# Seven block products in place of eight for the small terms of the last projection, in two more token groups of a GFNet + S2-MLP kernel

## The chip, the cores and the metric

The kernel runs on one core of a Trainium2 chip. The metric is the device time of one execution in microseconds (us); lower is better. The profile shown here is of one execution, and its engines are named PE (matmul), PEld (its weight load), DVE (vector), ACT (scalar), POOL (GpSimd) and SP (the queue that issues DMAs).

## The reference

The input is x, 2048 tokens by 448 features in float32. It is normalised by rows, and the output is x plus two branches on the normalised xn: a spectral filter, and a mixer with an MLP behind it.

```python
xn  = layernorm(x)
# A: global filter
yA  = irfft2(rfft2(xn) * (w_r + 1j*w_i))
# B: token shift, then MLP
h   = gelu(layernorm(xn) @ w1)                  # 448 -> 448
hs  = concat(h[:, 0:112] shifted +1, h[:, 112:224] -1, h[:, 224:336] +2, h[:, 336:448] -2)
x1  = xn + hs @ w2                              # 448 -> 448
yB  = x1 + gelu(layernorm(x1) @ w3) @ w4        # 448 -> 1792 -> 448
out = x + yA + yB
```

## The kernel before

**Split numbers.** All products run in float16 on operands split in two halves, hi and lo. A product of two split operands is three passes: hi by hi, hi by lo and lo by hi. The last two are the cross terms.

**The MLP.** The 2048 tokens stand in eight groups G of 256, and the 1792 hidden features in seven blocks fp of 256. A unit (G, fp) has a *front* (`front`, L434: 22 matmuls of 256 columns give h for 256 features and 256 tokens; then ACT takes the gelu at L772 and writes the hi half at L775, and DVE writes the lo half at L776 into the tile `hf`) and a *back* (`back`, L810: h times w4, summed in the PSUM tiles `acc` over the seven blocks). A plain back is 12 matmuls of 448 columns, 4 for each pass. `steps` is a generator that hands out fronts and backs in order, with fronts two units ahead; `run` takes from it. PSUM is taken by tags of two banks each: `mm`, `tr`, `sp` and `acc`.

**Block products.** `crossed(G, fp)` says which units form their cross terms another way; before, those of groups 5, 6 and 7 without (7, 5) and (7, 6). The cross term of a unit is a product of 2 by 2 blocks, and is made of seven block products of 128 tokens by 224 columns for each of its two passes, 14 matmuls in place of 8 of 448 columns. They need sums and differences of the blocks, here called forms: of h for each unit (`forms`, three DVE operations into the tile `hgm`, L785 to L787), and of w4 once for each block (`w4_forms`, POOL). Their sums go to four quarters of two more PSUM banks (`cr`, tag `tr`), which are added at the group's end by two ACT copies into `cross` (a part of `x2mem`) and six POOL or DVE additions.

**Around groups 1 and 2.** The same stretch also folds x for the spectral branch (`do_fold`: ACT, then four POOL operations on `xr` and `xf`), splits it (`step1_in`: `xh`, ACT hi and DVE lo, L594), multiplies it (`step1`: `ps` on PE at L603; ACT and DVE write `y`, L607 and L608), takes the largest magnitude of the filter (`w_scale`: eight loads of `wl` through two half buffers and eight DVE reductions `wm`, L269) and normalises the last four token blocks for group 6 and 7 (`ln2`: L537 to L552, tile `y`).

**What sets the order.** A tile scheduler orders each engine's instructions from priorities (`prio`; EVAC goes first, FILL last) and from hand-written lists: `behind(key)` holds an instruction in the order until another has been issued. `PACE`, `FOLD`, `WMAX` and `LATE` name for each step1 pair, fold, reduction and late normalisation the unit that it stands behind. Once built, each engine runs its own list in order, and a wait holds up all that stands behind it.

**The beginning.** Group 0 of 512 tokens goes through w1 (`w1_unit`: PE L464, ACT gelu L485, ACT hi L487, DVE lo L488, then a transposing DMA to the tile `h`, L491), and the shifted product with w2 (`w2_mm`, L509) reads those.

Of the kernel before, what the change touches and what calls it, by code (L numbers as in the profile page):

```python
# [31 lines left out]
AH = 2  # L32
PACE = [(0, 6), (1, 1), (1, 2), (1, 4), (1, 5), (2, 0), (2, 1), (2, 3)]
FOLD = [(0, 5), (1, 0), (1, 1), (1, 3), (1, 4), (1, 6), (2, 0), (2, 2)]
PIN = [("a3",), ("a3",), ("a3",), ("a3",)]
WMAX = [(1, 4), (1, 5), (2, 0), (2, 0), (2, 1), (2, 2), (2, 3), (2, 4)]
LATE = [(2, 2), (2, 3), (2, 4), (2, 5)]
HS = 3
STR = (5, 6, 7)
INV, LAG = 4, 2  # L40
EVAC, FILL = 0, 100000

# [80 lines left out]
def body(tc, nc, x, wf, w1, w2, w3, w4, c_g, c_n, c_small, out):  # L123
# [59 lines left out]
    warm = pc.tile([128, 1], F32, name="warm")  # L183
    V.memset(warm, 0.0)
    A.activation(out=warm, in_=warm, func=AF.Gelu_apprx_tanh)
    x2mem = pw.tile([128, 9 * F], F16, name="x2mem")
    wsrc = x2mem[:, 8 * F:8 * F + 512]
    V.memset(wsrc, 0.0)
    ones = pc.tile([128, 128], F32, name="ones")
# [33 lines left out]
    load_w3([2, 3])  # L223
    cross = x2mem.bitcast(F32)[:, 4 * F:4 * F + 2 * D].rearrange("p (i n) -> p i n", i=2)
    x2all = x2mem[:, 0:8 * F].rearrange("p (j t n) -> p j t n", j=4, t=7)
    w4raw = x2mem.bitcast(F32)[:, F:].rearrange("p (f n) -> p f n", f=14)
# [99 lines left out]
    def stats1(g, ks):  # L326
        if g not in mvs:
            mvs[g] = pc.tile([128, 4, 2], F32, name=f"mva{GRP[g][0]}")
        stats([xb(GRP[g][k]) for k in ks], f"a{GRP[g][ks[0]]}", mvs[g][:, ks[0]:])

    def norm1(g, apply, seen=0, mid=None):

        bs = GRP[g]
        n, b0 = len(bs), bs[0]
        stats1(g, range(seen, n))
# [140 lines left out]
    def w1_unit(g, i, pm=None):  # L476
        if pm is None:
            pm = bank(("tr" if g < 3 else "mm", "acc")[i // 2], f"pw1_{g}{i}")
            after["u", g, i] = (w1_in(g, [(i, pm)], range(4)).ins,)
        c = CS[GRP[g][i]]  # L480
        pm = pm[:, :D]
        pv_ = pm.rearrange("p (k n) -> p k n", k=4)
        h = hs_buf[c % (HS if g == 3 else HS + 2)]
        with behind(0, i - 2) if g == 0 and i > 1 else contextlib.nullcontext():
            A.activation(out=pm, in_=pm, func=AF.Gelu_apprx_tanh, scale=gsc[:, c:c + 1])  # L485
        with behind("a2") if g == 1 and i > 1 else contextlib.nullcontext():
            u = A.activation(out=h[:, 0, :, 0:112], in_=pv_, func=AF.Copy, scale=h1)  # L487
            v = V.scalar_tensor_tensor(out=h[:, 1, :, 0:112], in0=pv_, scalar=h1, in1=h[:, 0, :, 0:112],  # L488
                                       op0=ALU.mult, op1=ALU.subtract)
        o = h_at(g, i)  # L490
        d = SY.dma_start_transpose(out=hT[g][:, :, o:o + 128], in_=h.rearrange("p i k n -> p (i k n)"))  # L491
        after[g, i] = u.ins, v.ins
        after["h", g, i] = (d.ins,)
# [25 lines left out]
    def ln2(bs, engines, pins=None):  # L519
# [8 lines left out]
        for m in range(0, n, 2):  # L528
            w = stage(f"y{b0 + m}", 8 * 448, 0 if pins else (b0 + m) // 2 % 2, F16)
            o.append(w[:, 0:4 * D].bitcast(F32).rearrange("p (i n) -> p i n", i=2))  # L530
            y.append(w[:, 4 * D:8 * D].rearrange("p (i n) -> p i n", i=2))
            for i in range(2):
                e = engines[m + i]
                c = nm[:, m + i:m + i + 1]
                if e is A:
                    with behind("f", *pins[m + i]) if pins else contextlib.nullcontext():
                        A.activation(out=o[-1][:, i], in_=xb(b0 + m + i), func=AF.Identity, bias=c)  # L537
                else:
                    e.tensor_scalar(out=o[-1][:, i], in0=xb(b0 + m + i), scalar1=1.0, scalar2=c,
                                    op0=ALU.mult, op1=ALU.add)  # L540
# [27 lines left out]
    folds = {}  # L568

    def do_fold(b0):  # L570
        f = xf_buf[b0 // 2 % 4]
# [308 lines left out]
    def mlp(*args, **kw):  # L880
        run(steps(*args, **kw))
# [35 lines left out]
    def w4_split(f):  # L917
        split_w(w4p[0][:, 0, f:f + 2], w4p[0][:, 1, f:f + 2], w4raw[:, f:f + 2], s4)

    def w4_forms(fp):  # L920
        n, f = D // 2, 2 * fp
        b = [[w4p[0][:, :, f + r, n * c:n * c + n] for c in range(2)] for r in range(2)]
        m = w4all[:, 56 * 224:] if fp == 6 else w4x[:, 8 * 224 * fp:8 * 224 * (fp + 1)]
        m = m.rearrange("p (k n) -> p k n", n=224)
        t1 = [m[:, 6], m[:, 7]]
        t2, t3, t4 = (m[:, k:k + 4:3] for k in range(3))
        P.tensor_tensor(out=t3, in0=b[1][1], in1=b[0][1], op=ALU.add)
        for i in range(2):
            P.tensor_tensor(out=t1[i], in0=b[0][0][:, i], in1=b[0][1][:, i], op=ALU.subtract)
            P.tensor_tensor(out=t2[:, i], in0=b[1][1][:, i], in1=t1[i], op=ALU.subtract)  # L930
        P.tensor_tensor(out=t4, in0=b[1][0], in1=t2, op=ALU.subtract)
        w4f[fp] = [[x[:, i] for i in range(2)] for x in (b[0][0], b[1][0], b[1][1], t4)]
        w4f[fp] += [t1] + [[x[:, i] for i in range(2)] for x in (t2, t3)]

    def squares1():
        for t in range(4):
# [66 lines left out]
    with behind("a1"):  # L1003
        for k in range(4):
            w1_unit(0, k, first[k])
        n1.append(norm1(2, [P, V, A, V], 2))
    for k in (1, 3):
        with behind(0, 3):
            A.activation(out=w2p[:, 0, k], in_=w2s[:112, k], func=AF.Copy)
# [5 lines left out]
    turn(2)  # L1015
    for k in range(1, 4):
        w1_unit(1, k)
    for b, ks in ((0, (2, 0)), (1, (2, 0)), (2, (2, 0)), (3, (2,))):
        w2_mm(b, ks)
    with behind("w2p"):  # L1020
        n1[0][2]()
# [172 lines left out]
```

## Time and profile before

| | |
|---|---|
| median of 3 runs | 411.16 us (410.06 to 411.37) |
| the profiled execution | 409.13 us, of which its span is 407.0 us |
| PE busy | 401.7 us of the span (99%) |
| DVE, ACT, POOL busy | 303.6, 269.0, 178.8 us |
| granted TensorE clock | 0.999 |

PE is busy nearly from start to end. Its ends are modelled, so that one matmul of 448 columns is shown with 352 ns; how fast matmuls follow each other is read from the starts of rows of the timeline.

### The profile page before, as it was taken

To read this page: it belongs to the slowest core of one execution; us is meant where nothing else is said; L and a number is where in the kernel's file an instruction comes from. 1 tells how busy PE (TensorE), PEld (TensorE's weight loads), DVE (VectorE), ACT (ScalarE), POOL (GpSimd) and SP (SyncE) were. 2 spreads that over 40 slices of the span, in tenths; PEclk is the share of its full clock that TensorE was granted. 3 is DMA by queue.
4 is the path that set the end of the run, shared out by engine and by line. 5 is a ranking of instruction groups with operands and counts; after the bars stand their busy time and mean duration, and the time that the engine had idled before them with its cause. 6 is when DMAs were issued, how large, how long until landed. Compare 5 with 4: busy or idle time off the path is not lost.

```text
span 407.0 us, 8828 instructions
## 1 busy us (share of the span) xinstructions
PE 401.7 (99%) x3379; PEld 296.0 (73%) x3379; DVE 303.6 (75%) x658; ACT 269.0 (66%) x465; POOL 178.8 (44%) x276
## 2 busy tenths in 40 slices
PE   8999999999999999999999999999999999999996
PEld 3554555666767777776888888877788888888885
DVE  5988999898654757894577777763488879889545
ACT  4699993984838865863587888785956566544332
POOL 3889830011197747499243444441231254217100
PEclk9999999999999999999999999999999999999999
DMA  8999999906810374417055556642000022323201
GB/s 278 359 287 196 173 180 261 268 7 135 182 48 0 92 256 154 110 29 173 18 143 143 144 145 158 150 109 60 2 2 2 24 68 82 102 72 112 90 2 45
DMA packets 57209, 49.46 MB, mean 122 GB/s; under 512 B 41312, under 2 KB 52192, under 8 KB 57168
## 3 DMA queue, kind: packets, MB, share of 16 engines
q1 hardware_dynamic: 57168, 48.91, 46.1%
q8 instruction: 26, 0.43, 0.5%
q14 instruction: 15, 0.12, 0.1%
HBM read 35.06 MB, written 3.67 MB: 95 GB/s over the span
## 4 chain that ended last, share of the span: by engine, by line
PE 92%; DMA 3%; DVE 1%; POOL 1%; ACT 1%; issue 1%; SPq 0%; ACTq 0%
PE pw L434 32%; PE acc L810 24%; PE pw L509 6%; PE pw L464 6%; PE cr L825 4%; PE acc L825 3%; PE pu L706 3%; PE ps L603 3%; PE pp L660 2%; PE pe L726 2%; PE px L677 2%; PE py L748 2%; PE wps L888 2%; DMA h<-hs 2%; DMA x2mem<-w 1%; PE pta L413 1%
## 5 line engine op out<-in xcount | busy, mean ns | idle before, releaser
L434 PE MATMUL pw<-x2mem,w3p 128*128 128x256 f16 x1232 | 149.2, 272 | 0.0
L434 PEld LDWEIGHTS <-w3p 128*128 128x128 f16 x1232 | 118.8, 98 | 18.9
L810 PE MATMUL acc<-w4p,hf 128*128 128x448 f16 x508 | 107.4, 352 | 0.0
L810 PEld LDWEIGHTS <-hf 128*128 128x128 f16 x532 | 51.4, 98 | 35.5
L776 DVE SCALAR_TENSOR_TENSOR hf<-pw,h,hf 128x512 f16<-128x512 f32 x56 | 41.9, 748 | 36.6 <-ACT hf L775 36.4
L772 ACT ACTIVATE pw<-pw,pe 128x512 f32<-128x512 f32 x56 | 36.8, 657 | 44.6 <-PE pw L434 44.4
L509 PE MATMUL pw<-w2p,h 112*128 112x448 f16 x192 | 39.0, 352 | 0.3 <-DMA h<-hs 0.2
L775 ACT ACTIVATE hf<-pw,h 128x512 f16<-128x512 f32 x56 | 38.3, 684 | 1.3
L733 POOL TENSOR_TENSOR e<-e 128x226 f32<-128x226 f32 x16 | 11.2, 700 | 63.5 <-ACT e L730 60.2
L464 PE MATMUL pw<-w1p,w4x 128*128 128x448 f16 x176 | 34.9, 352 | 0.5 <-DVE h L966 0.5
L509 PEld LDWEIGHTS <-h 112*128 112x128 f16 x192 | 18.5, 99 | 17.2 <-DMA h<-hs 1.1
L687 POOL TENSOR_TENSOR xr<-te 128x450 f32<-128x450 f32 x16 | 15.7, 982 | 34.5 <-DVE te L685 34.5
L464 PEld LDWEIGHTS <-w4x 128*128 128x128 f16 x176 | 17.1, 98 | 16.4 <-ACT w4x L423 0.7
L695 POOL TENSOR_TENSOR zb<-xr,zb 128x450 f16<-128x450 f32 x16 | 16.2, 1011 | 16.8 <-ACT zb L694 16.1
L683 DVE SCALAR_TENSOR_TENSOR te<-px,sc,wc 128x450 f32<-128x450 f32 x16 | 11.0, 686 | 10.7 <-ACT te L682 5.9
L682 ACT ACTIVATE te<-px 64x450 f32<-64x450 f32 x32 | 17.3, 540 | 1.7 <-PE px L677 1.2
L718 ACT ACTIVATE U<-y 113x512 f16<-113x512 f16 x32 | 18.1, 621 | 0.1
L730 ACT ACTIVATE e<-pe 128x452 f32<-128x452 f32 x16 | 8.7, 546 | 13.9 <-PE pe L726 11.6
L740 ACT ACTIVATE vh<-e 128x448 f16<-128x448 f32 x16 | 9.2, 576 | 13.0 <-DVE e L738 12.8
L710 DVE SCALAR_TENSOR_TENSOR y<-pu,y 113x512 f16<-113x512 f32 x16 | 10.9, 688 | 6.9 <-ACT y L709 6.8
L582 POOL TENSOR_TENSOR xr<-xf 128x452 f32<-128x452 f32 x6 | 6.7, 1124 | 20.8 <-ACT xf L578 10.7
L741 DVE TENSOR_TENSOR vh<-e,vh 128x448 f16<-128x448 f32 x16 | 10.4, 653 | 7.1 <-ACT vh L740 7.1
(208 smaller groups left out, 793.6 us busy)
## 6 DMA issues: line engine op xcount, KB each, us to landing
wc<-wf SPq DMA_DIRECT2D x32, 225.0 KB, 3.7
wl<-wf SPq DMA_DIRECT2D x8, 450.0 KB, 3.9
xt<-x SPq DMA_DIRECT2D x3, 896.0 KB, 10.8
w3raw<-w SPq DMA_DIRECT2D x3, 896.0 KB, 14.1
xf<-x SPq DMA_DIRECT2D x6, 448.0 KB, 3.7
xr<-x SPq DMA_DIRECT2D x12, 224.0 KB, 2.5
out<-xr SPq DMA_DIRECT2D x12, 224.0 KB, 2.1
gn<-c_g SPq DMA_DIRECT2D x16, 128.0 KB, 3.2
```

The lines of the kernel that those rows point to most:

```text
L434: m = T.matmul(ps_out, wp[:, wi + t, cols], xT[:, xi + t, tok], start=t == 0 and wi + xi == 0, stop=t == 3 and wi == 4)
L464: m = T.matmul(pm[:, :D], xTs[g][:, xi + t, 128 * i:128 * i + 128], w1p[:, wi + t], start=t == 0 and p == 0, stop=t == 3 and p == 2)
L509: m = T.matmul(w2b[b][:, :D], hT[g][:112, 4 * hi + k, o:o + 128], w2p[:, wi, k], start=k == 2 and hi + wi == 0, stop=k == 3 and hi == 1)
L682: i = A.activation(out=e[64 * h:64 * h + 64], in_=px_[64 - 64 * h:128 - 64 * h, :2 * DF], func=AF.Copy)
L687: P.tensor_tensor(out=z, in0=t[:, 0], in1=t[:, 1], op=ALU.add)
L695: P.tensor_tensor(out=zv[1], in0=z, in1=zv[0], op=ALU.subtract)
L718: A.activation(out=U[b][:113, p].rearrange("p q (c k) -> p q c k", c=NC), in_=Y1[:113, p, :, :, b], func=AF.Copy)
L772: A.activation(out=pm, in_=pm, func=AF.Gelu_apprx_tanh, scale=r3)
L775: i = A.activation(out=h[:, 0], in_=pv_, func=AF.Copy, scale=h3)
L776: j = V.scalar_tensor_tensor(out=h[:, 1], in0=pv_, scalar=h3, in1=h[:, 0], op0=ALU.mult, op1=ALU.subtract)
L810: m = T.matmul(to, h[:, hi, 2 * f + i], w4p[0][:, wi, 2 * fp + f, r], start=fp == s and f == 0 and hi + wi == 0, stop=fp == e and f == 1 a ...
L825: m = T.matmul(to, h[:, hi, slot] if slot < 4 else g[:, hi, slot - 4], w4f[fp][k][wi], start=k in (0, 6) and fp == 0 and hi == 0, stop=hi ...
```

## The change

`STR` gets the groups 1 and 2, so 14 more units form their cross terms from seven block products. For that:

- the forms of w4 are made earlier and with four operations for each block in place of six: blocks 0 and 1 on POOL behind a normalisation step of block 8, blocks 2, 3 and 4 on POOL behind the first fold, blocks 5 and 6 on DVE behind unit (0, 6). Before, blocks 0 and 1 stood behind the first fold and 2 to 6 behind the last, all on POOL;
- the fronts of the two groups take PSUM from `mm` alone, but for the second, since `tr` now holds `cr`;
- the fourth fold buffer moves from `hgm` to `x2mem`, and is used once (`FBUF`);
- `WMAX` and `LATE` name later units, and the tail of the filter's scale stands behind (2, 6);
- in group 0, the first hi half of h stands ahead of the second gelu, the row statistics of group 2's tokens are spread between the lo halves, and the first products with w2 alternate between token blocks.

```diff
+FBUF = (0, 1, 2, 3, 0, 1, 2, 0)
-WMAX = [(1, 4), (1, 5), (2, 0), (2, 0), (2, 1), (2, 2), (2, 3), (2, 4)]
-LATE = [(2, 2), (2, 3), (2, 4), (2, 5)]
+WMAX = [(1, 5), (1, 6), (2, 2), (2, 3), (2, 4), (2, 4), (2, 5), (2, 5)]
+LATE = [(2, 2), (2, 3), (2, 5), (2, 6)]
-STR = (5, 6, 7)
+STR = (1, 2, 5, 6, 7)
...
-        with behind(0, i - 2) if g == 0 and i > 1 else contextlib.nullcontext():
+        with behind(0, max(i - 2, 0)) if g == 0 and i else contextlib.nullcontext():
             A.activation(out=pm, in_=pm, func=AF.Gelu_apprx_tanh, scale=gsc[:, c:c + 1])
...
-    def w4_forms(fp):
+    def w4_forms(fp, e):
...
-        t1 = [m[:, 6], m[:, 7]]
+        t1 = m[:, 6:8]
         t2, t3, t4 = (m[:, k:k + 4:3] for k in range(3))
-        P.tensor_tensor(out=t3, in0=b[1][1], in1=b[0][1], op=ALU.add)
-        for i in range(2):
-            P.tensor_tensor(out=t1[i], in0=b[0][0][:, i], in1=b[0][1][:, i], op=ALU.subtract)
-            P.tensor_tensor(out=t2[:, i], in0=b[1][1][:, i], in1=t1[i], op=ALU.subtract)
-        P.tensor_tensor(out=t4, in0=b[1][0], in1=t2, op=ALU.subtract)
+        for o, x, y, op in ((t3, b[1][1], b[0][1], ALU.add), (t1, b[0][0], b[0][1], ALU.subtract),
+                            (t2, b[1][1], t1, ALU.subtract), (t4, b[1][0], t2, ALU.subtract)):
+            e.tensor_tensor(out=o, in0=x, in1=y, op=op)
...
     with behind("a1"):
         for k in range(4):
             w1_unit(0, k, first[k])
-        n1.append(norm1(2, [P, V, A, V], 2))
+            if k < 2:
+                with behind(0, k):
+                    stats1(2, [k + 2])
+        n1.append(norm1(2, [P, V, A, V], 4))
...
-    for b, ks in ((0, (2, 0)), (1, (2, 0)), (2, (2, 0)), (3, (2,))):
+    for b, ks in ((0, (2,)), (1, (2,)), (0, (0,)), (2, (2,)), (1, (0,)), (2, (0,)), (3, (2,))):
         w2_mm(b, ks)
...
-    xf_buf.append(hgm.bitcast(F32).rearrange("p i n -> p (i n)")[:, 0:904].rearrange("p (b s d) -> p b s d", b=2, s=4))
+    xf_buf.append(x2mem.bitcast(F32)[:, 4 * F:4 * F + 904].rearrange("p (b s d) -> p b s d", b=2, s=4))
...
-    mlp([1, 2], ahead=AH, tags=("mm", "tr"))
+    gen = steps(range(1, 3), ahead=AH, tags=["mm", "tr"] + ["mm"] * 12)
     for b in range(0, NB, 2):
+        while ("m", *PACE[b // 2]) not in after:
+            run(gen, len(slots))
+        if b < 4:
+            with prio(FILL):
+                for fp in ((0, 1, 5, 6), (2, 3, 4))[b // 2]:
+                    with behind(*(("f", 0, 6) if fp > 4 else ("fold", 0) if b else ("ln", 8))):
+                        w4_forms(fp, V if fp > 4 else P)
         do_fold(b)
...
-    with prio(FILL):
-        for fp in range(7):
-            with behind("fold", 0 if fp < 2 else 14):
-                w4_forms(fp)
+    run(gen)
     ln2(range(12, 16), [A] * 4, LATE)
     with behind("X", 14):
         wm = w_scale()
     close("pfd")
-    with behind("m", 2, 5):
+    with behind("m", 2, 6):
         w_scale_end(wm)
```

How the instructions stand on DVE near the end of group 2, before. The rows run from the lo half of unit (2, 4) to that of unit (2, 6); `wm` is a reduction of the filter, `y14` a late normalisation, `y1` the lo half of a step1.

```order
L776 SCALAR_TENSOR_TENSOR hf24_1960<-pw3_24_1936,h3_713,hf24_1960 128x512
L269 TENSOR_REDUCE wm_2509<-wl_2510 128x1
L548 SCALAR_TENSOR_TENSOR y14_2477<-y14_2477,vs12_2471 128x64
L550 SCALAR_TENSOR_TENSOR y14_2477<-y14_2477,vs12_2471 128x384
L624 TENSOR_REDUCE wt_2528<-wm_2509 128x1
L776 SCALAR_TENSOR_TENSOR hf25_1999<-pw3_25_1975,h3_713,hf25_1999 128x512
L548 SCALAR_TENSOR_TENSOR y14_2477<-y14_2477,vs12_2471 128x64
L550 SCALAR_TENSOR_TENSOR y14_2477<-y14_2477,vs12_2471 128x384
L608 TENSOR_TENSOR y1_1510<-ps1_14_2385,y1_1510 128x128x4
L608 TENSOR_TENSOR y1_1510<-ps1_15_2400,y1_1510 128x128x4
L776 SCALAR_TENSOR_TENSOR hf26_2038<-pw3_26_2014,h3_713,hf26_2038 128x512
```

And now, on DVE from the lo half of unit (2, 5) to that of unit (2, 6); `hgm<-hf25` are the forms of that unit's h.

```order
L779 SCALAR_TENSOR_TENSOR hf25_2426<-pw3_25_2402,h3_713,hf25_2426 128x512
L270 TENSOR_REDUCE wm_2641<-wl_2642 128x1 x2
L611 TENSOR_TENSOR y1_1510<-ps1_14_2451,y1_1510 128x128x4
L551 SCALAR_TENSOR_TENSOR y14_2609<-y14_2609,vs12_2603 128x64
L553 SCALAR_TENSOR_TENSOR y14_2609<-y14_2609,vs12_2603 128x384
L788 TENSOR_TENSOR hgm_112<-hf25_2426 128x2x256
L611 TENSOR_TENSOR y1_1510<-ps1_15_2466,y1_1510 128x128x4
L627 TENSOR_REDUCE wt_2660<-wm_2641 128x1
L789 TENSOR_TENSOR hgm_112<-hf25_2426,hgm_112 128x2x128
L790 TENSOR_TENSOR hgm_112<-hf25_2426,hgm_112 128x2x128
L779 SCALAR_TENSOR_TENSOR hf26_2516<-pw3_26_2492,h3_713,hf26_2516 128x512
```

Two reductions have come between the lo half of (2, 5) and its forms, and the forms of (2, 5) stand behind both, behind a step1 and behind a normalisation. The back of (2, 5) on PE reads the forms.

On DVE again, where the first h of group 0 is written (`hs0`, `hs1` and `hs2` are its first three token blocks), before:

```order
L316 BN_STATS sta8_0_423<-xt2_78 128x6
L316 BN_STATS sta8_1_426<-xt2_78 128x6
L317 BN_AGGR mva6_349<-sta8_0_423 128x2
L488 SCALAR_TENSOR_TENSOR hs0_119<-pw1_00_222,h1_259,hs0_119 128x4x112
L317 BN_AGGR mva6_349<-sta8_1_426 128x2
L488 SCALAR_TENSOR_TENSOR hs1_120<-pw1_01_223,h1_259,hs1_120 128x4x112
L488 SCALAR_TENSOR_TENSOR hs2_121<-pw1_02_224,h1_259,hs2_121 128x4x112
```

And now, on DVE at the same place:

```order
L490 SCALAR_TENSOR_TENSOR hs0_119<-pw1_00_222,h1_259,hs0_119 128x4x112
L317 BN_STATS sta8_0_411<-xt2_78 128x6
L318 BN_AGGR mva6_349<-sta8_0_411 128x2
L490 SCALAR_TENSOR_TENSOR hs1_120<-pw1_01_223,h1_259,hs1_120 128x4x112
L317 BN_STATS sta9_0_418<-xt2_78 128x6
L490 SCALAR_TENSOR_TENSOR hs2_121<-pw1_02_224,h1_259,hs2_121 128x4x112
```

The first lo half no longer stands behind two row statistics; the second and third each stand behind one.

More of the change, by code (lines that the diff above doesn't have):

```diff
@@ L185, in body @@
     A.activation(out=warm, in_=warm, func=AF.Gelu_apprx_tanh)
-    x2mem = pw.tile([128, 9 * F], F16, name="x2mem")
+    x2mem = pw.tile([128, 9 * F + 16], F16, name="x2mem")
     wsrc = x2mem[:, 8 * F:8 * F + 512]
@@ L225, in body @@
     x2all = x2mem[:, 0:8 * F].rearrange("p (j t n) -> p j t n", j=4, t=7)
-    w4raw = x2mem.bitcast(F32)[:, F:].rearrange("p (f n) -> p f n", f=14)
+    w4raw = x2mem.bitcast(F32)[:, F:9 * F // 2].rearrange("p (f n) -> p f n", f=14)
     W4F = (0, 4, 8, 11, 14)
@@ L334, in norm1 @@
         n, b0 = len(bs), bs[0]
-        stats1(g, range(seen, n))
+        if seen < n:
+            stats1(g, range(seen, n))
         mv = mvs[g]
@@ L538, in ln2 @@
                 else:
-                    e.tensor_scalar(out=o[-1][:, i], in0=xb(b0 + m + i), scalar1=1.0, scalar2=c,
-                                    op0=ALU.mult, op1=ALU.add)
+                    j = e.tensor_scalar(out=o[-1][:, i], in0=xb(b0 + m + i), scalar1=1.0, scalar2=c,
+                                        op0=ALU.mult, op1=ALU.add)
+                    after["ln", b0 + m + i] = (j.ins,)
         V.tensor_scalar(out=a, in0=mv[:, :n, 1], scalar1=eps12, scalar2=None, op0=ALU.add)
@@ L570, in do_fold @@
     def do_fold(b0):
-        f = xf_buf[b0 // 2 % 4]
+        f = xf_buf[FBUF[b0 // 2]]
         X = f.rearrange("p b s d -> p (b s d)")[:, 0:2 * D + 2].rearrange("p (b d) -> p b d", b=2)
@@ L924, in w4_forms @@
         m = m.rearrange("p (k n) -> p k n", n=224)
-        t1 = [m[:, 6], m[:, 7]]
+        t1 = m[:, 6:8]
         t2, t3, t4 = (m[:, k:k + 4:3] for k in range(3))
-        P.tensor_tensor(out=t3, in0=b[1][1], in1=b[0][1], op=ALU.add)
-        for i in range(2):
-            P.tensor_tensor(out=t1[i], in0=b[0][0][:, i], in1=b[0][1][:, i], op=ALU.subtract)
-            P.tensor_tensor(out=t2[:, i], in0=b[1][1][:, i], in1=t1[i], op=ALU.subtract)
-        P.tensor_tensor(out=t4, in0=b[1][0], in1=t2, op=ALU.subtract)
+        for o, x, y, op in ((t3, b[1][1], b[0][1], ALU.add), (t1, b[0][0], b[0][1], ALU.subtract),
+                            (t2, b[1][1], t1, ALU.subtract), (t4, b[1][0], t2, ALU.subtract)):
+            e.tensor_tensor(out=o, in0=x, in1=y, op=op)
         w4f[fp] = [[x[:, i] for i in range(2)] for x in (b[0][0], b[1][0], b[1][1], t4)]
-        w4f[fp] += [t1] + [[x[:, i] for i in range(2)] for x in (t2, t3)]
+        w4f[fp] += [[x[:, i] for i in range(2)] for x in (t1, t2, t3)]
     def squares1():
```

## The prediction

> **What bounds the kernel now.** I read the page first, then what PE waited for, then rows of PE's timeline, and last DVE's prices.
>
> ```profile
> PE 401.7 (99%) x3379; PEld 296.0 (73%) x3379; DVE 303.6 (75%) x658; ACT 269.0 (66%) x465; POOL 178.8 (44%) x276
> PE 92%; DMA 3%; DVE 1%; POOL 1%; ACT 1%; issue 1%; SPq 0%; ACTq 0%
> ```
>
> ```profile
> PE wps L888 <- DVE x2mem L188: 1.2, 1, 1.2
> PE pw L464 <- DVE h L966: 0.5, 1, 0.5
> PE pw L509 <- DMA h<-hs: 0.2, 1, 0.2
> ```
>
> PE is the chain that ends last, and all its named waits are 1.9 us, the latest near 31 us. A busy PE need not be a fast one, since its ends are modelled. The starts decide:
>
> ```profile
> 128.88 2.57 PE L434 MATMUL pw<-x2mem,w3p 128*128 128x256 f16 x22
> 131.28 2.43 PE L810 MATMUL acc<-w4p,hf 128*128 128x448 f16 x12
> 133.55 0.27 PE L434 MATMUL pw<-x2mem,w3p 128*128 128x256 f16 x1
> ...
> 305.16 0.92 PE L810 MATMUL acc<-w4p,hf 128*128 128x448 f16 x4
> ...
> 306.78 0.26 PE L825 MATMUL acc<-w4p,hgm 128*128 128x224 f16 x1
> ...
> 307.26 0.73 PE L748 MATMUL py<-vh,csm 128*128 128x448 f16 x3
> ```
>
> A front takes 2.40 us (128.88 to 131.28). A plain back takes 2.27 us (131.28 to 133.55): 12 matmuls at 0.189 us. A crossed back takes 2.10 us (305.16 to 307.26): four at 0.189, so 0.76, and 14 in the other 1.34, at 0.096 each. The short matmuls cost half of the long ones, with nothing added. So PE streams columns without a gap. Columns taken away are time taken away, and any wait that is put in is time put in.
>
> **The change part by part.**
>
> *Fewer columns (PE, on the path).* Each of 14 backs goes from 2.27 to 2.10, so 14 x 0.17 = **-2.4 us**. The weight loads, six more for each unit, lie beside the matmuls:
>
> ```profile
> L825 PEld LDWEIGHTS <-hgm x152: 97/98/98, 300.7 to 396.5; 128*128 128x128 f16 x152
> ```
>
> A load of 98 ns is slightly longer than the 96 ns from one short matmul to the next, and the 0.096 already holds that. [...]
>
> *The first h.*
>
> ```profile
> 24.30 1.15 DVE L316 BATCH_NORM_STATS2 sta<-xt 128x6 f32<-128x448 f32 x2
> 25.45 0.65 DVE L488 SCALAR_TENSOR_TENSOR hs<-pw,h,hs 128x448 f16<-128x448 f32 x1
> 26.19 4.74 SPq L491 DMA_TRANSPOSE h<-hs  x3
> 31.30 7.04 PE L509 MATMUL pw<-w2p,h 112*128 112x448 f16 x34 [0.17 <-DMA h<-hs]
> ```
>
> The first lo half started at 25.45, behind two statistics; it now stands ahead of them, and its hi half ahead of a gelu. The transposes follow each other on SP, so an earlier first one pulls the next. PE lost at least 0.17 here, and the 34 matmuls span 6.69 from first to last start (7.04 less the 0.35 shown for one), 0.45 more than 33 x 0.189. I bound the gain by 0 and 0.6 and take **-0.3 us**, since the second block's lo half still stands behind a statistic and the order in which blocks are needed is the same.
>
> *New DVE work: the forms of h and of w4's last blocks.* Here are the prices, as least, median and most for `hgm` and `xh`, else as a mean:
>
> ```profile
> L785 DVE TENSOR_TENSOR hgm<-hf x19: 410/425/955, 291.1 to 392.4; 128x512 f16<-128x512 f16 x19
> L786 DVE TENSOR_TENSOR hgm<-hf,hgm x19: 276/287/670, 291.6 to 392.9; 128x256 f16<-128x256 f16 x19
> L787 DVE TENSOR_TENSOR hgm<-hf,hgm x19: 273/291/676, 291.9 to 393.2; 128x256 f16<-128x256 f16 x19
> L594 DVE TENSOR_TENSOR xh<-xf,xh x12: 614/1006/1487, 114.7 to 165.5; 128x452 f16<-128x452 f32 x12
> L776 DVE SCALAR_TENSOR_TENSOR hf<-pw,h,hf 128x512 f16<-128x512 f32 x56 | 41.9, 748 | 36.6 <-ACT hf L775 36.4
> L608 DVE TENSOR_TENSOR y<-ps,y 128x512 f16<-128x512 f32 x16 | 10.4, 681 | 1.8 <-ACT y L607 1.8
> L269 DVE TENSOR_REDUCE wm<-wl 128x1 f32<-128x900 f32 x8 | 8.6, 1080 | 1.1 <-DMA wl<-wf 1.1
> L834 DVE SCALAR_TENSOR_TENSOR xt<-acc,p,xt 128x448 f32<-128x448 f32 x12 | 8.1, 679 | 3.9 <-PE acc L810 3.4 <-PE acc L825 0.3
> L550 DVE SCALAR_TENSOR_TENSOR y<-y,vs 128x384 f16<-128x384 f32 x16 | 11.7, 733 | 0.0
> L548 DVE SCALAR_TENSOR_TENSOR y<-y,vs 128x64 f16<-128x64 f32 x16 | 5.9, 371 | 4.2 <-ACT y L547 4.2
> ```
>
> ```profile
> 140.00:160.00 20.00, 12.70 (x17) 1.00 0.57 192
> 160.00:180.00 20.00, 18.75 (x25) 1.00 0.35 94
> 180.00:196.00 16.00, 8.28 (x14) 1.00 0.53 120
> ```
>
> The three forms of a unit take 1.00 us at the medians. DVE has room for that from 140 to 160 us (12.70 of 20), but hardly from 160 to 180 (18.75 of 20). The change also moves six of eight reductions to units (2, 2) to (2, 5). So group 2 is where DVE can come late, and PE's last backs are where it shows, since no front stands between the backs of (2, 4), (2, 5) and (2, 6). I count there, from the end of front (2, 4).
>
> ```profile
> 181.36 2.43 PE L810 MATMUL acc<-w4p,hf 128*128 128x448 f16 x12
> 183.63 1.50 PE L603 MATMUL ps<-csm,xh 128*128 128x128 f16 x24
> 184.97 2.56 PE L434 MATMUL pw<-x2mem,w3p 128*128 128x256 f16 x22
> ```
>
> ```profile
> 182.98 0.75 DVE L776 SCALAR_TENSOR_TENSOR hf<-pw,h,hf 128x512 f16<-128x512 f32 x1 [0.72 <-ACT hf L775]
> ```
>
> ```profile
> DMA to landing us min/median/max: 3.2/3.9/5.0
> ```
>
> The last row is of the `wl` loads. PE's time until it needs the last form of (2, 5): back 2.10, front 2.40, back 2.10, a step1 pair 1.34 (183.63 to 184.97), front 2.40, back 2.10, and 1.62 into the back (305.16 to 306.78): 14.06 us. DVE's: 1.62 until it can start the lo half (181.36 to 182.98), lo 0.75, a reduction 1.08, then the next load of that half buffer 3.9, two reductions 2.16, a step1 half 0.68, a normalisation 1.10, forms and a step1 half 1.68: 12.97. DVE is 1.1 us early if it enters on time.
>
> It does not quite. In (2, 1), after the back of (1, 6), it evacuates twice (1.36), and does a lo half 0.75, forms 1.00 and two `xh`. That starts 2.10 after the front's end and must be over 6.12 after it (back, front, 1.62): with fast `xh` (0.61) 0.3 late, with median ones 1.1 late. Units (2, 2) and (2, 3) then bring 2 x (0.75 + 1.08 + 1.00 + 1.36 + 1.10) = 10.6 and two `xh`, 11.8 to 12.6, against two stretches of PE of 5.84 (back, step1, front): 0.1 to 0.9 more. So DVE enters 0.4 to 2.0 late, and the back of (2, 5) waits 0 to 0.9. Where it waits, (2, 6) waits some 0.5 more, since its forms stand behind the other half of the normalisation. I take 0.6 of these 0 to 1.4.
>
> The upper bound is from slowed rows. DVE operations on two SBUF tensors are longer while POOL works: `hgm` reaches 955 where its least is 410. [...] With forms at 1.26 (a fifth of the way to the largest, 2.30) and normalisations at 1.74 (the rows below, of the window from 116 to 196 us), DVE comes 4 x 0.26 and 3 x 0.64, so 3.0, later than at the medians: a wait of 3.9 in (2, 5), and 4.4 with (2, 6).
>
> ```profile
> L550 DVE SCALAR_TENSOR_TENSOR y<-y,vs 128x384 f16<-128x384 f32 x4 | 4.4, 1092 | 0.0
> L548 DVE SCALAR_TENSOR_TENSOR y<-y,vs 128x64 f16<-128x64 f32 x4 | 2.6, 646 | 1.3 <-ACT y L547 1.3
> ```
>
> ```profile
> 172.71 1.03 POOL L927 TENSOR_TENSOR w4x<-w4p 128x448 f16<-128x448 f16 x1
> ...
> 194.78 1.03 POOL L931 TENSOR_TENSOR w4p<-w4p 128x448 f16<-128x448 f16 x1
> ```
>
> I go by the lower end: those slow normalisations lay beside w4's forms on POOL, which ran from 172.71 to 195.8 and leave that stretch.
>
> *w4's forms.* On POOL, blocks 0 and 1 now run beside group 0, and 2 to 4 right ahead of the second fold. They are needed from the back of (1, 0) on. POOL sat idle for 8.5 us ahead of the first fold (last row below), which covers the first two; the three others delay the second fold by about 2 us, and its step1 pair had that to spare. The six-operation form is now four, each near 1.0. On DVE, blocks 5 and 6 are eight operations of about 0.4 (as `hgm`) in front of and between the two `xh` of the first step1 pair. With POOL running beside them they can make that pair wait: 0 to 0.9. For both I take **+0.3**.
>
> ```profile
> 109.95 1.06 POOL L582 TENSOR_TENSOR xr<-xf 128x452 f32<-128x452 f32 x1 [8.55 <-ACT xf L578]
> ```
>
> *Evacuation and PSUM.* The two ACT copies and six POOL additions for each group lie beside a front; the copies free `tr` within the 2.40 of the front that stands between. The fronts have two banks in place of four: a bank is asked for again 6.6 us later (back, front, back) and its evacuation takes 2.4 (1.62 and 0.75). Free, with 4.2 to spare; if DVE were later than that, this would wait too.
>
> *Sum.* -2.4 - 0.3 + 0.6 + 0.3 = -1.8. The profiled execution took 409.13 (407.0 of it the span), so it would take 407.3. The median of the runs, 411.16, lies 2.0 above that execution, and I forecast a median on the same footing: **409.4 us**.
>
> **The rivals.**
>
> *DVE becomes the bound at the end of group 2 (slower).* It needs the dearer prices above. The backs of (2, 5) and (2, 6) wait 4.4 us, and all else stays: 411.16 - 2.7 + 0.3 + 4.4 = 413.2. It turns the gain to a loss where all waits pass 2.7, and beyond 0.3% where they pass 3.9. For it: 18.75 of 20 busy before anything is added, and forms that stand behind two reductions whose load has only just been asked for. Against it: POOL has left w4's forms behind by then. Chance 0.22.
>
> *A wash.* At medians and a little above, the waits come to 1.5 to 3.9 us at two or three places and leave 410.0 to 412.3, say 410.9. Chance 0.24.
>
> *Weight loads pace the short matmuls (slower).* If a load of 0.098 were not hidden, a plain back would be 12 x 0.287 = 3.44 and a crossed one 4 x 0.287 + 14 x 0.194 = 3.86: 14 x 0.42 = 5.9 more, 417.1. [...] The rows at 305 us speak plainly against it. Chance 0.01.
>
> *The gain survives.* Waits of at most 1.4: 408.4 to 409.9. Chance 0.53.
>
> **Numbers.** A measurement of this kernel tells about 0.3%, 1.2 us, from no change. Faster by more: 0.53; within: 0.24; slower by more: 0.23. The range reaches from 407.6 (all gained, no wait, and runs 0.6 lower) to 412.8.
>
> **What would show it.** A crossed back in groups 1 and 2 of 2.10 us, with 112 matmuls of 448 columns less and 196 of 224 more in all. Right: PE's list of waits has no row for `hgm` or `xh` above a few tenths. Wrong: PE waiting for DVE at L828 near 186 to 192 us, at the block products of (2, 5) or (2, 6), or at L606 near 118 us; or fronts of group 2 waiting for `mm`. The first h is right if the wait at L511 near 31 us is gone.

## The result and the profile after

The changed kernel takes 425.39 us as a median of six runs (422.96 to 426.39), beside 410.61 for the kernel before on the same chip. The ratio is 1.0335, with a 95% interval of 1.0305 to 1.0365: 13.8 us slower by the ratio, 14.8 by the two medians. I had forecast 409.4 and a range up to 412.8.

The profiled execution took 422.96 us (span 420.9, 13.9 more than before) and is the fastest of the six. Its busy times and its chain, from the page:

```profile
PE 403.4 (96%) x3463; PEld 305.6 (73%) x3463; DVE 340.6 (81%) x708; ACT 269.7 (64%) x469; POOL 179.6 (43%) x266
PE 68%; DVE 21%; issue 5%; DMA 3%; ACT 2%; SPq 0%; DVEq 0%
```

POOL is as busy as before. DVE has 50 operations more, but 37 us more of busy time, and a fifth of the chain. What PE waited for (us in total, times, longest):

```profile
PE ps L606 <- DVE xh L597: 4.7, 4, 1.8
PE acc L813 <- DVE hf L779: 4.1, 2, 2.3
PE ps L606 <- DVE y L611: 2.8, 1, 2.8
...
PE cr L828 <- DVE hf L779: 0.4, 1, 0.4
```

(Lines moved: L606 was L603, L813 was L810, L828 was L825, L779 was L776, L597 was L594, L611 was L608, and the forms L788 to L790 were L785 to L787.) The two waits for the lo half `hf` fall at 105 and 112 us, inside *group 0*, where the change crosses nothing. Products of step1 wait near 124 and 126 (the first pair), 142, 149 and 182 us.

The same stretch of DVE in both executions, before and after, while PE headed for the first of these waits:

```profile
103.13 0.61 DVE L550 SCALAR_TENSOR_TENSOR y<-y,vs 128x384 f16<-128x384 f32 x1
103.66 0.15 DVE L303 TENSOR_TENSOR nqb<-nib 128x4 f32<-128x4 f32 x1
103.85 0.16 DVE L304 TENSOR_TENSOR nqb<-nqb,vb 128x4 f32<-128x4 f32 x1
103.95 0.75 DVE L776 SCALAR_TENSOR_TENSOR hf<-pw,h,hf 128x512 f16<-128x512 f32 x1
```

```profile
102.68 0.96 DVE L304 TENSOR_TENSOR nqb<-nib 128x4 f32<-128x4 f32 x1
103.57 1.13 DVE L551 SCALAR_TENSOR_TENSOR y<-y,vs 128x64 f16<-128x64 f32 x1
104.62 1.40 DVE L553 SCALAR_TENSOR_TENSOR y<-y,vs 128x384 f16<-128x384 f32 x1
105.95 0.98 DVE L305 TENSOR_TENSOR nqb<-nqb,vb 128x4 f32<-128x4 f32 x1
106.85 0.74 DVE L779 SCALAR_TENSOR_TENSOR hf<-pw,h,hf 128x512 f16<-128x512 f32 x1
```

And POOL beside the latter:

```profile
97.20 4.31 POOL L932 TENSOR_TENSOR w4x<-w4p 128x448 f16<-128x448 f16 x4
101.48 0.22 POOL L529 TENSOR_SCALAR nm<-mvb 128x4 f32<-128x4 f32 x1
101.69 0.94 POOL L541 TENSOR_SCALAR y<-xt,nm 128x448 f32<-128x448 f32 x1
102.59 4.32 POOL L932 TENSOR_TENSOR w4x<-w4p,w4x 128x448 f16<-128x448 f16 x4
```

An operation on four columns, 0.15 us before, takes 0.96: about one of POOL's operations (4.31 / 4 = 1.08). The lo half reads PSUM and keeps its 0.75. Where DVE runs such small operations one behind the other (the inverse square root and the normalisation of a row block), most of those beside a POOL operation pay (seven of them took 0.90 to 1.02 us each between 99 and 114 us), and the lo half that stands behind them is late.

The third reading is PE's own speed after a pause. Columns: busy time and count of PE, PEld, DVE, ACT, POOL, then the granted clock.

```profile
115.50:119.00 3.50, 3.50 (x12) 1.43 (x10) 3.50 (x5) 0.00 (x0) 3.50 (x4) 0.54 0.46 130
184.50:187.50 3.00, 3.00 (x28) 2.90 (x29) 3.00 (x6) 1.47 (x3) 0.00 (x0) 0.51 0.26 76
```

After the waits of 2.3 and 2.8 us the clock was 0.54 and 0.51 over these stretches, so each of the two cost about 1.6 more. From the starts of successive matmuls, pauses and slow stretches together are 22.1 us after and 5.9 before. The 16.2 more, less the 2.4 of columns saved, are 13.8 of the 13.9 us. The places add up to it: by the starts, 4.4 us at the two lo halves, 3.5 at the first step1 pair, 1.9 near 142 and 149, 3.0 at 182 and 3.2 in the two slow stretches come to 16.0.

Theory A: what costs the time is a DVE operation on SBUF tensors being held for a whole POOL operation beside it. Theory B: DVE has too much work by its own length, or the order is at fault.

### The profile page after: what moved, and what is told of

It is laid out like the page before. It is cut to its first block, busy times and chain, and to the rows that moved or that the text cites. A ratio compares the mean times of both kernels' runs of the same rounds, so it can differ in the third digit from the quotient of the medians.

```text
span 420.9 us, 9090 instructions
## 1 busy us (share of the span) xinstructions
PE 403.4 (96%) x3463; PEld 305.6 (73%) x3463; DVE 340.6 (81%) x708; ACT 269.7 (64%) x469; POOL 179.6 (43%) x266
## 4 chain that ended last, share of the span: by engine, by line
PE 68%; DVE 21%; issue 5%; DMA 3%; ACT 2%; SPq 0%; DVEq 0%
PE pw L436 20%; PE acc L813 11%; PE pw L511 8%; PE pw L466 8%; PE cr L828 3%; DVE xh L597 3%; DVE hf L779 3%; PE pu L709 3%; PE acc L828 2%; PE pp L663 2%; PE px L680 2%; PE wps L891 2%; PE ps L606 2%; DVE hgm L788 2%; DVE xr L562 1%
## 5 line engine op out<-in xcount | busy, mean ns | idle before, releaser
L436 PE MATMUL pw<-x2mem,w3p 128*128 128x256 f16 x1232 | 150.8, 273 | 0.0
L813 PE MATMUL acc<-w4p,hf 128*128 128x448 f16 x396 | 88.6, 358 | 4.2 <-DVE hf L779 4.1
L813 PEld LDWEIGHTS <-hf 128*128 128x128 f16 x420 | 40.9, 99 | 31.3 <-DVE hf L779 5.0
L779 DVE SCALAR_TENSOR_TENSOR hf<-pw,h,hf 128x512 f16<-128x512 f32 x56 | 41.6, 744 | 23.0 <-ACT hf L778 20.1
L828 PEld LDWEIGHTS <-hgm 128*128 128x128 f16 x264 | 25.4, 99 | 0.2
L828 PE MATMUL cr<-w4x,hgm 128*128 128x224 f16 x174 | 25.1, 261 | 0.0
L828 PEld LDWEIGHTS <-hf 128*128 128x128 f16 x198 | 18.7, 98 | 6.1 <-DVE hf L779 0.7
L610 ACT ACTIVATE y<-ps 128x512 f16<-128x512 f32 x16 | 9.1, 590 | 19.6 <-PE ps L606 19.5
L606 PE MATMUL ps<-csm,xh 128*128 128x128 f16 x192 | 14.2, 230 | 7.5 <-DVE xh L597 4.7
```

The lines of the kernel that those rows point to most:

```text
L436: m = T.matmul(ps_out, wp[:, wi + t, cols], xT[:, xi + t, tok], start=t == 0 and wi + xi == 0, stop=t == 3 and wi == 4)
L606: T.matmul(pm[:, 128 * q:128 * q + 128], t[:, o:o + 128], cR[ri][:, 128 * (q % 2):128 * (q % 2) + 128], start=n == 0, stop=n == 2)
L779: j = V.scalar_tensor_tensor(out=h[:, 1], in0=pv_, scalar=h3, in1=h[:, 0], op0=ALU.mult, op1=ALU.subtract)
L813: m = T.matmul(to, h[:, hi, 2 * f + i], w4p[0][:, wi, 2 * fp + f, r], start=fp == s and f == 0 and hi + wi == 0, stop=fp == e and f == 1 a ...
L828: m = T.matmul(to, h[:, hi, slot] if slot < 4 else g[:, hi, slot - 4], w4f[fp][k][wi], start=k in (0, 6) and fp == 0 and hi == 0, stop=hi ...
```

## The experiments

**Taking the change apart.** Four kernels. `first_h` is the kernel before with the part of the change that concerns group 0's first h. `forms_only` and the two others are the changed kernel with:

```diff
# forms_only
-STR = (1, 2, 5, 6, 7)
+STR = (5, 6, 7)
# no_w4: in w4_forms, nothing is computed
-            e.tensor_tensor(out=o, in0=x, in1=y, op=op)
+            pass
-        w4f[fp] = [... t4)] ... (t1, t2, t3)]
+        w4f[fp] = [[x[:, i] for i in range(2)] for x in (b[0][0], b[1][0], b[1][1], b[0][1], b[0][0], b[1][0], b[1][1])]
# no_w4_h: that, and in forms()
-        if crossed(G, fp):
+        if crossed(G, fp) and G < 3:
+            hg[G, fp] = hs[G, fp]
+        elif crossed(G, fp):
```

> The kernel before, with the changed first h order alone (statistics of the third tile group behind the first two gelus, hi half of the first block not held back, first products of w2 interleaved). PE's waits at L509 near 31 to 36 us go, and PE reached the same place 0.8 to 0.9 us earlier in the changed kernel. Expected 0.9 us less than before, 409.7 (409.2 to 410.4). The rival, that the earlier start is eaten up again by a later wait: within 0.2 us of before.

> The changed kernel with groups 1 and 2 not crossed (STR without 1 and 2): w4's forms still made in the first group, first h order and reductions as changed. Theory A, that POOL's early forms of w4 make each DVE operation beside them wait for a whole POOL operation: PE's waits at 105 and 112 us with the half-speed matmuls behind them (6.1 us) and those at L606 near 124 us behind DVE's own w4 forms (3.5 us) stay, less 0.9 for the first h: 419 (417 to 421). Theory B, that DVE simply has too much work once h's forms are added in groups 1 and 2: only the eight w4 forms on DVE are left, 410 to 414.

> The changed kernel without any forms of w4: the block products read blocks of w4 itself in their place (that part of the product is wrong), so POOL and DVE do not make them at all. h's forms and the products stay. Theory A: the waits at 105, 112 and 124 us go, 9.6 us with the half-speed matmuls; those near 142, 148 and 182 us (6.8 us) stay in part, since folds still run on POOL beside h's forms: 416 (413 to 418). Theory B: the waits at 105 and 112 us come from the order on DVE and stay; only DVE's eight forms (about 3.5 us) go: 420 to 423.

> As the kernel without w4's forms, and in groups 1 and 2 without h's forms too: the products read h itself in their place (that part is wrong). What stays of the change is PE's own saving, the evacuation through ACT and POOL, the moved reductions and the first h order. Both theories: before less 2.4 (columns) less 0.9 (first h), 407.3 (406.5 to 408.5). If the evacuation or the two banks of mm cost something, it is above 408.5, with PE waits for mm or for tr in the trace.

| kernel | median, us | ratio to before (95%) | us from before, by the ratio |
|---|---|---|---|
| `first_h` | 410.48 | 1.0007 (0.9988 to 1.0026) | +0.3 |
| `no_w4_h` | 408.19 | 0.9936 (0.9910 to 0.9962) | -2.6 |
| `no_w4` | 413.03 | 1.0061 (1.0039 to 1.0083) | +2.5 |
| `forms_only` | 419.75 | 1.0224 (1.0193 to 1.0256) | +9.2 |
| the change | 425.39 | 1.0335 (1.0305 to 1.0365) | +13.8 |

Without any new forms the change is 2.6 us faster, near the 2.4 of the columns. h's forms cost 5.1 (from -2.6 to +2.5), w4's forms 11.3 (from +2.5 to +13.8), and without any new product w4's forms alone still cost 9.2. `forms_only` is where theory A put it and far from theory B. `no_w4` is at the low end of A, 3 us under the 416. I had counted the 9.6 us in the profiled execution, the fastest, and taken them off the median, 425.39; between the two profiled executions lie 10.35 us (422.96 and 412.61).

`first_h` gains nothing, a miss. Its first transposes were issued 1.1 us earlier than before (25.08, not 26.19), but took longer. First that kernel, then the changed one:

```profile
25.08 7.55 SPq L492 DMA_TRANSPOSE h<-hs  x3
```

```profile
25.08 4.70 SPq L493 DMA_TRANSPOSE h<-hs  x3
```

In the profiled execution of `first_h` PE then stood 2.1 us at the first product with w2, which started at 33.07, after the three had ended at 32.63; in `no_w4_h` the three took 5.86 and PE's two waits for `h` 0.6. The earlier issue is real; the landing varies between executions (the three took 4.70 to 7.55 us in these), and over 12 runs nothing is left.

**The cost by itself.** A kernel of its own, without the reference's work: DVE operations of one kind, with POOL idle or busy with one kind.

> Not the kernel, but a measurement by itself: 35 sections, in each six DVE operations of one kind while POOL is idle or runs operations of one kind back to back. DVE: an F32 product of 128x4, a scaling of 128x4, a difference of 128x512 F16, the normalisation of 128x384, xh's difference of 128x452, a lo half from PSUM, a maximum over 128x900. POOL: sums of 128x448 F16 as w4's forms, the same at 128x112, sums of 128x452 F32 as a fold, a scaling of 128x448. The output is zeros. Theory A: a DVE operation on two SBUF tensors waits for the whole POOL operation beside it, so the product of 128x4 goes from 0.16 to about 1 us beside POOL's 448 columns and to 0.3 or 0.4 beside 112 columns; the lo half from PSUM and the maximum stay at 0.75 and 1.08. Rival: the two engines share bandwidth, so that DVE's time grows in proportion to what it reads, and the product of 128x4 stays below 0.25.

DVE's operations, as least, median and most of 30 (in ns):

```profile
L43 DVE TENSOR_TENSOR o<-a,b x30: 149/155/1105, 4.8 to 35.9; 128x4 f32<-128x4 f32 x30
L44 DVE TENSOR_SCALAR o<-a x30: 157/164/1114, 41.6 to 72.5; 128x4 f32<-128x4 f32 x30
L45 DVE TENSOR_TENSOR o<-a,b x30: 411/421/1357, 78.2 to 116.2; 128x512 f16<-128x512 f16 x30
L48 DVE TENSOR_TENSOR o<-a,b x30: 617/627/1562, 168.6 to 212.5; 128x452 f16<-128x452 f32 x30
L49 DVE SCALAR_TENSOR_TENSOR o<-pm,k,b x30: 740/743/746, 217.9 to 255.2; 128x512 f16<-128x512 f32 x30
L51 DVE TENSOR_REDUCE o<-a x30: 1078/1080/1082, 257.9 to 299.0; 128x1 f32<-128x900 f32 x30
```

The lo half from PSUM (L49) and the maximum over one SBUF tensor (L51) stay within 6 ns. The others are held, and by the length of POOL's operation, not by their own size: the product of four columns goes from 0.149 to 1.105. (That is one of six in its section; the others had run, or begun, before POOL's sums.) The difference of 512 columns, first beside POOL's 112 columns, then beside its 452:

```profile
L56 POOL TENSOR_TENSOR po<-pa,pb 128x112 f16<-128x112 f16 x13 | 5.6, 461 | 0.0
L45 DVE TENSOR_TENSOR o<-a,b 128x512 f16<-128x512 f16 x5 | 2.6, 575 | 0.0
```

```profile
L57 POOL TENSOR_TENSOR po<-pa,pb 128x452 f32<-128x452 f32 x5 | 6.4, 1315 | 0.0
L45 DVE TENSOR_TENSOR o<-a,b 128x512 f16<-128x512 f16 x4 | 5.2, 1355 | 0.0
```

The same difference, 411 ns at the least, takes 575 on average beside POOL's operations of 461, and 1355 beside those of 1315. The rival of shared bandwidth is out: four columns would not have paid 0.95 us.

**Where w4's forms hurt.** Three kernels: `quarters` cuts POOL's forms of blocks 0 and 1 into quarters; `late01` makes them behind the first fold; `x_first` puts DVE's blocks 5 and 6 behind the first `xh` pair.

```diff
# quarters, in short: for POOL and blocks 0 and 1
-            e.tensor_tensor(out=o, in0=x, in1=y, op=op)
+            for k in range(2):
+                s = slice(112 * k, 112 * k + 112)
+                for i in range(2):
+                    e.tensor_tensor(out=o[:, i, s], in0=x[:, i, s], in1=y[:, i, s], op=op)
# late01, in short: the key that blocks 0 and 1 stand behind
-    with behind("ln", 8):
+    with behind("fold", 0):
# x_first, in short: the key that blocks 5 and 6 stand behind
-    with behind("f", 0, 6):
+    with behind("x", 1):
```

> The changed kernel, with POOL's early forms of w4's blocks 0 and 1 cut into quarters (112 columns each, 32 operations in place of eight; same work, same place, nearly the same order on DVE). Theory A: what a DVE operation waits is one POOL operation, now a quarter as long, so DVE's eight operations of 128x4 fall from about 0.95 to about 0.3, and PE's waits at 105 and 112 us, with the half-speed matmuls 6.1 us, fall below 2: 421 (419.5 to 423). Theory B, that the order or the amount of work makes DVE late: nothing changes, 424.5 to 426.

> The changed kernel with w4's blocks 0 and 1 made on POOL behind the first fold, where the kernel before makes them, in place of ahead of it; blocks 2 to 4 follow, so the second fold comes some 9 us later on POOL. Theory A: the waits at 105 and 112 us go (6.1 us); the second step1 pair, which already waited 0.8 us, waits up to 3 us more for its fold: 421 (419 to 423). Theory B: 424 to 428, since the same work only moves later.

> The changed kernel with DVE's forms of w4's blocks 5 and 6 behind the first xh pair in place of in front of it. The waits of the first step1 pair near 124 and 126 us (3.5 us) go; the forms, nine to ten us of DVE, then stand ahead of the first pair's evacuation and h's forms of (1, 0), which are 2 us late at the most: 422.5 (421 to 425). If DVE has no time at all to spare between 125 and 150 us, the wait only moves: 425 to 426.

Measured: 421.08 (ratio 1.0257, 1.0209 to 1.0304), 421.22 (1.0244, 1.0196 to 1.0293) and 422.61 (1.0284, 1.0242 to 1.0326): the first two where theory A said, the third where its expectation, which names no theory, had it. In `quarters` the same small operation of DVE, in the same place:

```profile
104.05 0.35 DVE L305 TENSOR_TENSOR nqb<-nqb,vb 128x4 f32<-128x4 f32 x1
104.32 0.74 DVE L779 SCALAR_TENSOR_TENSOR hf<-pw,h,hf 128x512 f16<-128x512 f32 x1
```

0.35 in place of 0.98, the lo half 2.5 us earlier, and the waits at 105 and 112 us are gone. Not all of it is kept: PE comes to the first step1 pair earlier now and waits there 4.9 us in all, by the starts of its matmuls, where it waited 3.5. `late01` lost the two waits too, but gave time back at another place than I had expected: not at the second step1 pair (0.3 us by the starts), but at the first, where a slow stretch lasted twice as long as either in the changed kernel (granted clock 0.5 from 120.6 to 127.5 us). So its number is in part luck. In `x_first` the first pair no longer waits, and the back of (1, 0) waits some 2.7 us, by the starts, for h's forms instead.

**h's forms, and a version that would beat both.** `no_w4_short` is `no_w4` with the folds cut into quarters; `all_short` is `x_first` with all of POOL's forms and folds cut so; `g2` crosses group 2 alone of the two, all forms of w4 on POOL, one block behind each fold from the third on, with `WMAX` and `LATE` as before.

```diff
# no_w4_short and all_short: the four sums of a fold as sixteen
-        P.tensor_tensor(out=u[:, 0], in0=ad, in1=bc, op=ALU.add)
+        for m in range(4):
+            r = m // 2, m % 2
+            P.tensor_tensor(out=u[:, 0, r[0], r[1]], in0=ad[:, r[0], r[1]], in1=bc[:, r[0], r[1]], op=ALU.add)
...
# g2, beside the early forms taken out
-STR = (1, 2, 5, 6, 7)
+STR = (2, 5, 6, 7)
+        with prio(FILL), behind("fold", b):
+            for fp in ((0, 1), (), (2,), (3,), (4,), (5,), (6,), ())[b // 2]:
+                w4_forms(fp, P)
```

> The kernel without w4's forms (block products read blocks of w4 in their place, that part is wrong), with POOL's folds cut into quarters: sixteen operations of 113 columns for each pair of rows in place of four of 452; same work, same place. Without the cut it took 413.0 and PE lost 6 us at the step1 pairs and at the end of group 1. Theory A, that h's forms and xh are late there because each waits for a whole POOL operation of the fold: they wait for a quarter now, PE's waits fall to 2 to 3 us: 410 (408.5 to 411.5). Theory B, that h's forms are simply too much work for DVE in groups 1 and 2: 412.3 to 413.7, or above it since POOL's folds take half as long again.

> The changed kernel, correct in full, with all that shortened a wait: DVE's forms of w4's blocks 5 and 6 behind the first xh pair, and all of POOL's forms of w4 and its folds cut into quarters. From 422.6 with the first alone: less 4.5 for the early forms and 2 to 4 for the folds: 415 (412 to 418) under theory A; 421 to 424 under theory B. It beats the kernel before only if DVE's forms cost nothing, which neither theory says.

> An attempt at a version that beats both: only group 2 is crossed beside 5, 6 and 7 (STR = 2, 5, 6, 7), w4's blocks 0 and 1 made behind the first fold as before, one more block behind each fold from the third on, all on POOL, reductions and normalisations where before has them. It saves 7 x 0.17 = 1.2 us on PE. h's forms of one group cost half of what both cost, 2.5; POOL's forms now lie beside group 1 and 2's xh. Expected 412 (410 to 415); below 409.5 only if DVE has room for seven units' forms after all.

Measured: 413.89 (1.0068, 1.0026 to 1.0109), 418.07 (1.0218, 1.0186 to 1.0249) and 416.02 (1.0146, 1.0122 to 1.0169). `all_short` is just outside theory A's 412 to 418 and below theory B's; `g2` is outside its range. `no_w4_short` reads like theory B, but its runs lie 5.4 us apart (409.57 to 415.01), and its trace shows one DVE operation that did not wait for a quarter of a fold, but for nearly a whole fold. First DVE, then POOL:

```profile
158.82 5.39 DVE L793 TENSOR_TENSOR hgm<-hf 128x512 f16<-128x512 f16 x1
```

```profile
157.68 2.92 POOL L588 TENSOR_TENSOR xr<-xf 128x113 f32<-128x113 f32 x8
160.55 2.76 POOL L593 TENSOR_TENSOR xf<-xr 128x113 f32<-128x113 f32 x8
```

A form of 0.42 lasted 5.39 while POOL ran short operations without a gap (the fold's sixteen, then one addition of 224 columns). `all_short` has the same at an `xh` pair, 1.24 us for both where nothing holds them:

```profile
117.38 7.34 DVE L602 TENSOR_TENSOR xh<-xf,xh 128x452 f16<-128x452 f32 x2 [3.97 <-ACT xh L601]
```

In `quarters`, operations as short and as close held others for one of them only (DVE's operations on four columns took 0.31 to 0.36 us between 100 and 105 us); what makes the difference is not shown. So cutting POOL's work is no sure cure, and `no_w4_short` decides nothing between A and B. `g2` lost 5.8 us by the medians, against the 1.7 expected. PE stood longest at the end of group 1, for the evacuation of `acc`, which stood on DVE behind an `xh` pair slowed by folds and forms:

```profile
PE acc L813 <- DVE xt L837: 3.6, 1, 3.6
```

The last kernel therefore takes away what DVE waits for and leaves DVE's work: `no_w4`, with each fold replaced by fills, which read nothing, behind one sum of two columns.

```diff
-        P.tensor_tensor(out=u[:, 0], in0=ad, in1=bc, op=ALU.add)
-        P.tensor_tensor(out=u[:, 1], in0=ad, in1=bc, op=ALU.subtract)
-        ...
+        i = P.tensor_tensor(out=X[:, :, D:D + 1], in0=X[:, :, 0:1], in1=X[:, :, D - 1:D], op=ALU.add)
+        for k in range(9):
+            t = xr[:, 452 * (k % 2):452 * (k % 2) + 452] if k < 8 else f.rearrange("p b s d -> p (b s d)")[:, 2 * D + 2:]
+            with tc.issue_after(i.ins):
+                i = P.memset(t, 0.0)
```

> The kernel without w4's forms, and with POOL's folds replaced by work of about the same time that reads nothing: eight fills of 452 columns in place of four sums (the spectral part is wrong, and w4's forms are not made). DVE's operations are the same in number and size as in the kernel without w4's forms, which took 413.0; with h's forms left out too it took 408.2. [...] Theory B, that h's forms are too much work for DVE by their own length: 412 to 414.

Theory A gave this kernel 408 us (407 to 409.5), theory B 412 to 414. Measured: 406.51 us, ratio 0.9902 (0.9879 to 0.9925), half a microsecond below theory A's range. All fourteen units' forms are on DVE, as many and as large as in `no_w4`, and PE does not wait for them. `xh` in the changed kernel, in `no_w4` and here:

```profile
L597 DVE TENSOR_TENSOR xh<-xf,xh x14: 610/1370/1567, 123.7 to 190.4; 128x452 f16<-128x452 f32 x14
```

```profile
L597 DVE TENSOR_TENSOR xh<-xf,xh x14: 613/622/1483, 113.5 to 181.5; 128x452 f16<-128x452 f32 x14
```

```profile
L598 DVE TENSOR_TENSOR xh<-xf,xh x14: 620/624/1081, 110.0 to 173.7; 128x452 f16<-128x452 f32 x14
```

The medians of the last two are alike; what shrinks from `no_w4` is the longest, 1483 to 1081, and above all the forms. Their second operation from 110 to 200 us, in `no_w4` and here:

```profile
L789 DVE TENSOR_TENSOR hgm<-hf,hgm x14: 278/593/1176, 123.6 to 196.1; 128x256 f16<-128x256 f16 x14
```

```profile
L790 DVE TENSOR_TENSOR hgm<-hf,hgm x14: 282/284/741, 124.0 to 189.2; 128x256 f16<-128x256 f16 x14
```

All three forms and `xh` together took DVE some 11 us less than in `no_w4`, as the same operations. The fills, with their busy time and mean (ns):

```profile
L589 POOL MEMSET xr<- 128x452 f32 x63 | 26.7, 476 | 0.0
```

Theory B is out for h's forms too: their own length fits. What does not fit is their length beside POOL's sums. The order on DVE moved somewhat between these two kernels, so the 6.5 us between them are not all proven to come from POOL's sums; that no count of work on DVE stands in the way is. POOL was also done sooner: the fills took it 28.9 us, the folds of `no_w4` 34.2, and what that gave is not measured apart. Why this one is 1.7 below `no_w4_h` stays open.

No version that computes everything beats the kernel before.

## Why the prediction was wrong

- *Fewer columns, -2.4:* right. `no_w4_h`, which keeps little else, is 2.6 faster (1.6 to 3.7), and a back of group 1 in the changed kernel, from 139.47 to 141.57 us, takes the 2.10.
- *The first h, -0.3:* the lower bound, 0. The wait near 31 us is gone in the changed kernel's trace, but comes back in other executions with the landing of the transposes.
- *w4's forms, +0.3 (0 to 0.9):* the step that failed, at +9.2 alone. "POOL sat idle for 8.5 us ahead of the first fold (last row below), which covers the first two" asks only whether POOL has time. I did not look at what DVE ran there, from 99 to 109 us before: four normalised row blocks and an inverse square root in small steps, with group 0's lo halves between them. I had the slowed rows, and put a price on them in group 2 alone. The operations on four columns, too small to be in any term, cost some 0.8 us each where they were held (0.96 and 0.98 in place of 0.15 and 0.16), and PE lost 4.4 us at the two lo halves and 1.7 by the clock. The forms on DVE, counted "about 0.4", took 0.88 to 1.22 beside POOL's three blocks (all but the last, 0.38), and the first step1 pair waited 3.5, not 0 to 0.9. Of the signs of being wrong, the wait of that pair came (named near 118 us, found at 124 and 126); one at L828 near 186 to 192 us, or for `mm`, did not.
- *The wait at the end of group 2, 0.6 (0 to 1.4):* mis-sized and misplaced. PE stood 2.8 us at L606 (182 us) for `y`, which stood on DVE behind a slow `xh` pair (2.98), a lo half, a reduction and two forms; I had looked at the block products of (2, 5). Two more pairs waited some 2 us together near 142 and 149, where "DVE has room": from 140 to 160 us it is busy for 19.26 of 20 now, in place of 12.70 (the first row below). My reason for the lower end, that w4's forms leave POOL there, held for the normalisations (0.60 us at 185 and 188 us), but forgot the folds: they stay, and DVE is slow beside them too (`xh` 1.37 us at the median, 0.61 at the least). So it is beside the additions below, which stand with the slow pair: POOL's two sums at the end of group 1, from the term that I called free.

```profile
140.00:160.00 20.00, 18.45 (x198) 16.00 (x196) 19.26 (x27) 13.72 (x26) 11.25 (x11) 1.00 0.22 59
```

```profile
177.45 2.98 DVE L597 TENSOR_TENSOR xh<-xf,xh 128x452 f16<-128x452 f32 x2
```

```profile
176.19 2.34 POOL L852 TENSOR_TENSOR xt<-xt,x2mem 128x448 f32<-128x448 f32 x2
178.63 1.31 POOL L585 TENSOR_TENSOR xr<-xf 128x452 f32<-128x452 f32 x1
```

- *Evacuation and PSUM, free:* right within some tenths for PE and the banks (`no_w4_h` shows 0.3 and 0.2 at the end of group 1), but not for DVE beside POOL's additions, as above.
- *The price of a wait:* I took it as its length. Two of the waits, of 2.3 and 2.8 us, cost some 1.6 us more each by the clock, which no term had.
- *The rival that DVE becomes the bound* named the engine and the side; its 413.2 came from one place, and there were five.

## What to carry to other kernels

Before work goes to an idle POOL, list what DVE runs beside it by operands, not by length: here each kind of DVE operation on two SBUF tensors in the measurement by itself, and the scaling of one, reached 1.11 to 1.56 us beside POOL's (0.15 to 0.62 at the least), and a chain of tiny ones paid most (0.15 us became 0.96). Cutting POOL's operations shortened the usual wait here (0.98 us to 0.35 in `quarters`), but short ones without a gap once held a DVE operation for nearly all of them (5.39 us). When an engine turns up late, ask what it is held by before counting its work: here h's forms fitted, as many and as large, once POOL ran fills in place of its folds (406.51 us in place of 413.03).

## What the runs showed of the hardware that I had not expected

- A DVE operation can be held for far longer than one POOL operation: 5.39 us beside a fold of sixteen sums of 113 columns, for 0.42 alone. The length of one POOL operation, which fits the measurement by itself (1.36 us beside 1.32), does not cover it. The measurement by itself shows the same the other way round: a POOL copy of one column, 0.20 us at 25.34 us of the same trace, took 3.22 us while DVE ran six differences without a gap:

```profile
171.85 3.32 DVE L48 TENSOR_TENSOR o<-a,b 128x452 f16<-128x452 f32 x6
172.00 3.22 POOL L73 COPY s<-s 128x1 f32<-128x1 f32 x1 [2.78 <-DVE s L72]
```

- A scaling of four columns with a single SBUF tensor was held too (164 ns, at most 1114), a maximum over 900 columns was not (1078 to 1082).
- The granted clock fell to a half at long pauses of PE. By the waits of the profile it did so at 2.8 us in the changed kernel (182 us), at 3.1 in `forms_only`, 3.6 in `g2`, 4.6 in `no_w4_short` and 6.3 in `all_short`. Of the waits of 2.2 to 2.4 it followed some (2.3 in the changed kernel at 112 us, 2.2 twice in `x_first`) and not others (2.3 in `forms_only`, 2.2 in `no_w4` and in `quarters`), and in the changed kernel none of 1.8 and less. It stayed at a half for 3.4 us each time in the changed kernel, and for 6.8 in `forms_only` from 124.6 us on. In `x_first` a mean clock of 0.987 over 421.1 us makes some 10.9 us at a half, more than the 3.5 and 3.4 after its two waits; what brought the rest, and what sets the limit, is not shown.
